# Moving the last step of the row statistics behind the next tile's work, and a segment's shifts to where the segment is loaded

## The chip, the cores and the metric

The kernel runs on one core of one Trainium2 chip. The core has five engines that run their own instruction queues side by side, each in the order in which its queue was filled: PE (TensorE, the matrix multiplies), DVE (VectorE), ACT (ScalarE), POOL (GpSimd) and SP (SyncE, which here issues most of the loads and stores between the chip's memory and the core). PE's partial sums lie in PSUM, whose banks DVE and ACT read and free; here eight banks are taken in turn. An engine that comes to an instruction whose input is not ready, or whose output space is not free, stands still, with everything behind it in its queue.

The metric is the device time of one execution in microseconds. Lower is better.

## The reference

Four layers work on one sequence of 2048 rows of 640 numbers, in the order A, B, A, B. Each reads the layer-normalised rows and adds its result to the rows:

```
def _layernorm(x):  m = mean(x); v = var(x); return (x - m) / sqrt(v + 1e-5)

x = x + _A_ref(_layernorm(x), A_wqkv, A_wo)
x = x + _B_ref(_layernorm(x), B_wq, B_wk, B_wv, B_wo, B_beta)
x = x + _A_ref(_layernorm(x), ...)
x = x + _B_ref(_layernorm(x), ...)
```

A is linear attention with 32 heads of 20: `phi(q) @ (sum of phi(k) v)` over all rows, divided by `phi(q) @ (sum of phi(k))`, and a projection with `wo`. B cuts the rows into four segments of 512: softmax attention within a segment under a causal mask, mixed by a gate with a linear-attention memory of the segments before it, and a projection. Of all this the change touches one thing, the layer normalisation of the rows that a layer has just written. With r = (v + 1e-5)^-0.5 a normalised row is x*r + (-m*r). The kernel calls r `rs`, the second term, the shift, `nb` (or `nb4` for four tiles at once), and the normalised tile `xh`.

## The kernel before, in words

A segment of 512 rows is worked on as four tiles of 128 rows. Only PE's order is written out by hand: Python generators are woven into one another, each yields a cost, and PE's instructions stand in the order in which the generators issued them. The orders of the other engines are set by a scheduler, which goes by the order of issue and by its own estimates of when things are ready. `issue_after(x)` makes what is issued under it, on the engine of instruction x, stand behind x.

*Layer A.* `g_first` builds keys, queries and memory, and `merge` folds the projections. For a segment, `a_head` prepares, and `a_second` then runs over the four tiles: it loads the old rows (`xo`, L340), multiplies the tile by the output weights in two halves of 15 matmuls (`o_half`, L406), and after each half DVE adds the old rows (`xn`, L483). When both halves are there, `moments` (L343 to L355) makes the statistics: DVE's two `bn_stats` (L348) and `bn_aggr` (L350), DVE's `rs = var + 1e-5` (L352), POOL's power -0.5 (L353), and DVE's `nb` (L355). `normed` lets ACT make `xh` (L378). Two tiles later `turn` transposes `xh` on PE (L329), and ACT (L333) and DVE (L334) copy it as a high and a low half into `xT`, the input of layer B. The turns of the last two tiles are the generator `tail`, which is woven into B's projections.

*Layer B.* `b_project` makes values (w_Bv, L406), queries and keys (w_Bq, w_Bk, L391; split by ACT L830 and DVE L831), `pkT` (DVE L431, turned on PE in L858) and the memory's sums (L868). Attention of the segments runs woven into all of this: scores with DVE's row maxima (PE L993, DVE L999), the maxima split and turned (L1008, L1009, L1017, ACT L1019, SP L1022), scores again for the exponentials (PE L1034, ACT L1038), weights times values (L1061) and normalisation (L1074, L1077). `p_read` brings A's prepared query tiles back (`pqi`, L744, L754 to L760) to be turned on PE.

`b_out` is B's counterpart of `a_second`. Here ACT scales a half (L480) and POOL adds the old rows (L481). When another layer follows, DVE's `gather` (L363, L364) takes the statistics of the tile before, after the last tile `settle` makes `rs` of the whole segment (DVE L370, POOL L371) and `nb4` (DVE L373), and `load_segment` later loads the four tiles again for the next layer's `g_norms`.

*Where the work stands.* Layer by layer, `a_second` of segment s is woven with B's memory work of segment s-1; segment s's projections are woven with the tail, with `a_head` of the next segment and, from s = 2 on, with `b_out` of segment s-2. In time, in the first pair of layers: `a_second` of segment 0 from 262 us, of segment 1 from 340 us, of segment 2 from 478 us and of segment 3 from 633 us; `b_out` of the four segments between 540 and 970 us. The second pair repeats the `a_second` part from 1092 us on, with no `b_out` that takes statistics, since no layer follows. So `nb` runs 36 times (4 in the opening, 32 in `a_second`), `nb4` 7 times (3 in the opening, 4 in `b_out`).

Of the kernel before, what the change touches and what calls it, by code (L numbers as in the profile page):

```python
# [9 lines left out]
F32 = mybir.dt.float32  # L10
# [4 lines left out]
OP = mybir.AluOpType  # L15
# [6 lines left out]
P = 128  # L22
C = D // P
SEG = 512
NSEG = S // SEG
NT = SEG // P
# [103 lines left out]
def pause(n):  # L130
    for _ in range(n):
        yield 0.0
# [12 lines left out]
class Kernel:  # L145
# [194 lines left out]
        self.nc.sync.dma_start(x, src[r:r + P])  # L340
        return x

    def moments(self, x):  # L343

        nc, sb = self.nc, self.sb
        st = sb.tile([P, 2, 6], F32, tag="st", name="st", bufs=3)
        for k in range(2):
            nc.vector.bn_stats(st[:, k], x[:, k * HN:(k + 1) * HN])  # L348
        mv = sb.tile([P, 2], F32, tag="mv", name="mv", bufs=4)
        nc.vector.bn_aggr(mv, st)  # L350
        rs = sb.tile([P, 1], F32, tag="rs", name="rs", bufs=4)
        self.taken = nc.vector.tensor_scalar(rs, mv[:, 1:2], 1e-5, None, op0=OP.add)  # L352
        self.power = nc.gpsimd.tensor_tensor(rs, rs, self.mhalf, op=OP.pow)  # L353
        nb = sb.tile([P, 1], F32, tag="nb", name="nb", bufs=4)
        self.last = nc.vector.tensor_scalar(nb, mv[:, 0:1], rs, -1.0, op0=OP.mult, op1=OP.mult)  # L355
        return x, nb, rs

    def gather(self, x, mv):
# [4 lines left out]
            nc.vector.bn_stats(st[:, k], x[:, k * HN:(k + 1) * HN])  # L363
        nc.vector.bn_aggr(mv, st)  # L364

    def settle(self, mv):

        nc, sb = self.nc, self.sb
        rs = sb.tile([P, NT], F32, tag="rs4", name="rs4", bufs=NSEG)
        nc.vector.tensor_scalar(rs, mv[:, :, 1], 1e-5, None, op0=OP.add)  # L370
        nc.gpsimd.tensor_tensor(rs, rs, self.mhalf.to_broadcast([P, NT]), op=OP.pow)  # L371
        nb = sb.tile([P, NT], F32, tag="nb4", name="nb4", bufs=NSEG)
        nc.vector.scalar_tensor_tensor(nb, mv[:, :, 0], -1.0, rs, op0=OP.mult, op1=OP.mult)  # L373
        return rs, nb

    def normed(self, x, nb, rs):
# [98 lines left out]
    def o_half(self, oT, wo, L, x, xn, n, later=False, begun=None):  # L475
        nc = self.nc
        p = self.proj_n(oT, wo, 0, n, begun, range(3, C)) if begun is not None else self.proj_n(oT, wo, 0, n)
        c = slice(n * HN, (n + 1) * HN)
        if later:
            nc.scalar.activation(xn[:, c], p, AF.Copy, scale=self.io[L])  # L480
            nc.gpsimd.tensor_tensor(xn[:, c], xn[:, c], x[:, c], op=OP.add)  # L481
        else:
            nc.vector.scalar_tensor_tensor(xn[:, c], p, self.io[L], x[:, c], op0=OP.mult, op1=OP.add)  # L483


    def parts(self, xh, xs, i):
# [7 lines left out]
    def norms(self, src, s, box, gap):  # L494

        x = [self.load_x(src, s, i) for i in range(NT)]
        mv = self.sb.tile([P, NT, 2], F32, tag="mv4", name="mv4", bufs=2)
        with self.tc.issue_after(self.keyed.ins) if s == 1 else nullcontext():
            for i in range(NT):
                self.gather(x[i], mv[:, i])  # L500
            rs, nb = self.settle(mv)
        box.append([(x[i], nb[:, i:i + 1], rs[:, i:i + 1]) for i in range(NT)])
        yield 0.0
        yield from pause(gap)
        yield from self.g_norms(s, box, 4 if s == 1 else 0)

    def load_segment(self, src, s, box, st):

        rs, nb = st["norm"]
        box.append([(self.load_x(src, s, i), nb[:, i:i + 1], rs[:, i:i + 1]) for i in range(NT)])  # L510
        yield 0.0

# [265 lines left out]
    def a_second(self, src, dst, s, L, box, norm):  # L778


        nc = self.nc
        o, oT = box["o"], box["oT"]
        xT = self.x_t() if norm else None
        xh = []
        for i in range(NT):
            if i + 3 < NT:
                yield from self.p_read(L, s, i + 3, o)
            x = self.load_x(src, s, i, "xo")
            xn = self.row("xn")
            t = iter(())  # L790
            if i + 1 < NT:
                oT.append(self.new_oT())
                t = self.turn(o[i + 1], oT[i + 1], 0)
            for n in range(2):
                yield from (c for c in [next(t, None)] if c)
                self.o_half(oT[i], L["wm"], "G", x, xn, n)
                yield self.COST_N
            r = s * SEG + i * P
            self.q_x.dma_start(dst[r:r + P], xn)
            if norm:  # L800
                if i > 1:
                    yield from self.turn(xh[i - 2], xT, i - 2)
                xh.append(self.normed(*self.moments(xn)))
        box["xT"] = xT

        def tail():
            for i in range(NT - 2, NT):
                yield from self.turn(xh[i], xT, i)
        box["tail"] = tail()


# [112 lines left out]
    def b_out(self, st, wo, src, dst, norm):  # L924

        yield lambda: st.get("attended")
        nc, s = self.nc, st["s"]
        made = []
        mv = self.sb.tile([P, NT, 2], F32, tag="mv4", name="mv4", bufs=2) if norm else None

        def load(i):
            if st["o"] is None and i < NT:
                read.append(self.row("ol"))
                nc.sync.dma_start(read[i], st["od"][i])

        def turned(i):
            load(i + 1)
            o = read[i] if st["o"] is None else st["o"][:, i]
            oT.append(self.new_oT())
            return self.turn(o, oT[i], 0)  # L940

        oT, read, begun = [], [], [None, None]
        load(0)
        t = turned(0)
        if st.get("ends"):
            ahead = turned(1)
            yield next(t)
            yield next(ahead)
            for n in range(2):
                begun[n] = self.proj_n(oT[0], wo, 0, n, cs=range(3))  # L950
                yield 9 * HN * COL
        yield from t
        for i in range(NT):
            x = self.load_x(src, s, i, "xo")
            xn = self.row("xn")
            t = iter(()) if i + 1 == NT else ahead if i == 0 and st.get("ends") else turned(i + 1)
            for n in range(2):
                yield from (c for c in [next(t, None)] if c)
                self.o_half(oT[i], wo, "B", x, xn, n, later=not st.get("ends"), begun=begun[n] if i == 0 else None)
                yield self.COST_N  # L960
            r = s * SEG + i * P
            self.q_x.dma_start(dst[r:r + P], xn)
            made.append(xn)
            if norm and i > 0:
                self.gather(made[i - 1], mv[:, i - 1])
        if norm:
            self.gather(made[-1], mv[:, NT - 1])
            st["norm"] = self.settle(mv)


    def stacks(self, st, g):
# [256 lines left out]
    def dense(self, layers, stage_ctx):  # L1228
# [15 lines left out]
        while i < n:  # L1244
# [35 lines left out]
            if last:  # L1280
                self.rate = R_END
                segs[-1]["ends"] = True
                yield from chain(fin, *out)
            else:
                self.rate = R_MID
                for k in "kq":
                    wA[k] = self.fetch(("A", k))
                L = self.g_begin(i + 2)
                src = xs[i + 2]
                x = [[] for _ in range(NSEG)]  # L1290
                loads = lambda s: self.load_segment(src, s, x[s], segs[s])
                norms = lambda s: self.g_norms(s, x[s])
                over = lambda st: lambda: st.get("attended")
                yield from weave(fin, chain(loads(0), norms(0)))
                use = lambda n: wA[n]
                yield from weave(self.g_first(0, x[0], use, L, over(segs[2])),
                                 chain(loads(1), when(segs[2], "attended", out[2]), norms(1)))
                yield from weave(self.g_first(1, x[1], use, L, over(segs[3])),
                                 chain(when(segs[3], "attended", out[3]), loads(2), norms(2)))
                yield from weave(self.g_first(2, x[2], use, L), chain(loads(3), pause(8), norms(3)))  # L1300
                wA["v"] = self.fetch(("A", "v"))
                yield from weave(self.g_first(3, x[3], use, L), self.a_head(L, 0, box))
# [63 lines left out]
```

## Time and profile before

| | us |
|---|---|
| median of three runs (lowest to highest) | 1705.25 (1703.31 to 1706.91) |
| the profiled execution | 1704.55 |
| its span | 1702.8 |
| PE busy | 1637.9 (96% of the span) |
| DVE busy | 1272.3 (75%) |
| ACT busy | 994.2 (58%) |
| POOL busy | 505.9 (30%) |

The span runs from the first to the last instruction in the trace; 1.75 us of the execution lie outside it. Row numbers such as L355 are lines of the kernel before. In a view of groups a row gives line, engine, operation, output<-input, count, then busy time, mean in ns of one, then the idle time of the engine just ahead of such instructions and what ended it. In a timeline a row gives start and duration in us, and in brackets the idle time ahead of it with what released it. In a table of stretches, a row gives the stretch, its length, and then busy time with the number of instructions for PE, PE's weight loads, DVE, ACT and POOL, the granted PE clock (1.00 is full speed), the share of time of the transfers and their GB/s.

### The profile page before, as it was taken

The page shows a single profiled execution, that of the slowest core. Times are in us where ns is not written, and L with a number is a line of the kernel's source. Part 1 is how long each engine was busy: PE and PEld are TensorE (multiplying, and loading weights), DVE is VectorE, ACT ScalarE, POOL GpSimd, SP SyncE. Part 2 cuts the span into 40 slices and gives each one's busy share as a digit, 9 for nine tenths or more (in the row PEclk, how much of TensorE's full clock was granted, in tenths as well). Part 3 has the DMA queues.
Part 4 walks back from the last instruction along what each step waited for, and adds up shares of the span by engine and source line. Part 5 has one row for each costly group of instructions (what it writes and reads, how often), then busy time and mean ns, then how long its engine had stood idle before and what let it go on. Part 6 is the DMA issues. An engine that isn't in the chain of part 4 may idle for free.

```text
span 1702.8 us, 37843 instructions
## 1 busy us (share of the span) xinstructions
PE 1637.9 (96%) x13788; PEld 1018.6 (60%) x13788; DVE 1272.3 (75%) x4015; ACT 994.2 (58%) x1888; POOL 505.9 (30%) x1046
## 2 busy tenths in 40 slices
PE   7999979999999999999999999999999999999998
PEld 5767757554465556556566777765546545645555
DVE  7888887487887788759874465847888978878773
ACT  6666533347756746667776454333675676666673
POOL 3442222013223322333452210310322332233452
PEclk9999989999999999999999999999999999999999
DMA  6424654421322331353211303423232323323432
GB/s 218 151 75 169 223 203 152 136 98 59 111 79 69 115 118 56 128 183 95 72 56 39 117 32 125 178 94 123 70 110 89 114 83 110 102 86 111 140 103 95
DMA packets 110372, 191.00 MB, mean 112 GB/s; under 512 B 14172, under 2 KB 69596, under 8 KB 107624
## 3 DMA queue, kind: packets, MB, share of 16 engines
q1 hardware_dynamic: 97704, 142.68, 25.9%
q0 software_dynamic: 3264, 24.91, 4.1%
q10 hardware_dynamic: 9216, 20.98, 3.2%
q8 instruction: 109, 1.79, 0.4%
q14 instruction: 79, 0.65, 0.1%
HBM read 109.32 MB, written 78.64 MB: 110 GB/s over the span
## 4 chain that ended last, share of the span: by engine, by line
PE 66%; DVE 17%; ACT 9%; issue 3%; DMA 3%; POOL 2%; SPq 0%; ACTq 0%; POOLq 0%; DVEq 0%
PE ps L406 25%; PE ps L391 13%; PE ps L1061 8%; PE ps L580 4%; PE ps L1034 4%; ACT pe L1038 3%; PE ps L993 3%; PE ps L329 3%; DVE ps L999 3%; PE ps L457 2%; PE ps L1074 1%; DVE e L421 1%; DVE wmx L243 1%; DVE split L270 1%; DVE xT L334 1%
## 5 line engine op out<-in xcount | busy, mean ns | idle before, releaser
L999 DVE CUSTOM_DVE_ANT_0 ps<-ps,maskw 128x512 f32<-128x512 f32 (+3 forms) x1024 | 472.0, 518 | 28.7 <-PE ps L993 25.9
L1038 ACT ACTIVATE pe<-ps,lsc 128x512 f32<-128x512 f32 x640 | 395.4, 696 | 63.0 <-PE ps L1034 59.8
L406 PEld LDWEIGHTS <-xT 128*128 128x128 f16 x2880 | 282.2, 99 | 115.0 <-issue 6.2
L1045 POOL TENSOR_SCALAR_AFFINE_SELECT pe<-pe 128x256 f32<-128x256 f32 (+1 forms) x640 | 233.4, 372 | 350.5 <-ACT pe L1038 342.7
L406 PEld LDWEIGHTS <-oT 128*128 128x128 f16 x1920 | 184.5, 98 | 84.7 <-issue 8.3
L1061 PE MATMUL ps<-pe,v 128*32 128x512 f32 (+3 forms) x2048 | 161.6, 436 | 8.8 <-DVE oT L334 1.9
L406 PE MATMUL ps<-wm,oT 128*128 128x320 f16 x960 | 141.3, 299 | 3.8 <-DVE rs L352 2.6
L406 PE MATMUL ps<-w_Bo,oT 128*128 128x320 f16 x960 | 141.5, 299 | 3.2 <-ACT oT L333 2.0
L406 PE MATMUL ps<-w_Ak,xT 128*128 128x320 f16 x960 | 140.6, 303 | 3.1 <-DVE xT L334 1.0
L406 PE MATMUL ps<-w_Bv,xT 128*128 128x320 f16 x960 | 142.3, 303 | 0.2
L391 PE MATMUL ps<-xT,w_Bq 128*128 128x512 f16 x600 | 140.9, 379 | 1.3 <-ACT pe L1038 0.8
L999 DVE DVE_READ_ACCUMULATOR2_ANT mg<- 128x1 f32 x1024 | 142.1, 139 | 0.1
L580 PE MATMUL ps<-pk,xs 128*128 128x321 f16 (+1 forms) x960 | 140.7, 304 | 1.1 <-DVE pk L543 0.7
L391 PE MATMUL ps<-xT,w_Bk 128*128 128x512 f16 x600 | 138.5, 379 | 1.2 <-ACT pe L1038 1.2
L406 PE MATMUL ps<-w_Aq,xT 128*128 128x320 f16 x960 | 137.6, 299 | 0.1
L993 PE MATMUL ps<-ks,qs 60*128 60x512 f16 (+3 forms) x1024 | 123.5, 297 | 7.6 <-ACT pe L1038 3.5
L580 PEld LDWEIGHTS <-xs 128*128 128x128 f16 x960 | 93.9, 99 | 41.0 <-issue 1.6
L421 DVE SCALAR_TENSOR_TENSOR e<-e,r 128x320 f32<-128x320 f32 x128 | 69.6, 544 | 53.6 <-ACT r L420 53.0
L1034 PE MATMUL ps<-qs,ks 62*128 62x512 f16 (+3 forms) x1024 | 105.6, 300 | 2.1 <-ACT pe L1038 1.1
L1061 PEld LDWEIGHTS ps<-pe,v 128*32 128x32 f32 x2048 | 65.4, 109 | 68.7 <-issue 40.9
L831 DVE SCALAR_TENSOR_TENSOR nat<-ps,nat 128x512 f16<-128x512 f32 x80 | 55.2, 690 | 62.6 <-ACT nat L830 62.3
L391 PEld LDWEIGHTS <-w_Bk 128*128 128x128 f16 x600 | 57.1, 98 | 66.5 <-issue 6.4
(202 smaller groups left out, 2359.6 us busy)
## 6 DMA issues: line engine op xcount, KB each, us to landing
x<-xn ACTq DMA_DIRECT2D x48, 320.0 KB
qs<-qd SPq DMA_DIRECT2D x128, 120.0 KB
ks<-kd SPq DMA_DIRECT2D x128, 120.0 KB
xo<-x SPq DMA_DIRECT2D x48, 320.0 KB
pqi<-pqd SPq DMA_DIRECT2D x32, 320.0 KB
qd<-nat SPq DMA_DIRECT2D x40, 256.0 KB
kd<-nat SPq DMA_DIRECT2D x40, 256.0 KB
x<-in_A_x SPq DMA_DIRECT2D x16, 320.0 KB
```

Of the source, the lines that this page charges most:

```text
L329: nc.tensor.transpose(pt[:, (c - c0) * P:(c - c0 + 1) * P], src[:, c * P:(c + 1) * P], self.ident)
L391: nc.tensor.matmul(p, w[:, c, a, t * P:(t + 1) * P], xT[:, c, b, :], start=k == 0, stop=k == 3 * C - 1)
L406: nc.tensor.matmul(p, xT[:, c, a, i * P:(i + 1) * P], w[:, c, b, n * HN:(n + 1) * HN], start=k == 0, stop=k == 3 * C - 1)
L421: nc.vector.scalar_tensor_tensor(e, e, 1.0, r, op0=OP.min, op1=OP.add)
L580: nc.tensor.matmul(p, xs[:, i, a, c * P:(c + 1) * P], pk[i][:, b, cols], start=i == 0 and a == b, stop=i == NT - 1 and a == 1)
L831: nc.vector.scalar_tensor_tensor(nat[:, 1], p, QK_SHIFT, nat[:, 0], op0=OP.mult, op1=OP.subtract)
L993: nc.tensor.matmul(bs[par][:, a:a + n], qs[r, p, i * P:(i + 1) * P], ks[r, p, :n], start=True, stop=True)
L999: nc.vector.tensor_tensor_reduce(bs[par][:, a:a + n], bs[par][:, a:a + n], self.maskw[:, SEG - n:], 1.0, NEG, OP.add, OP.max, G["mg"][:, p ...
L1034: nc.tensor.matmul(b[:, a:a + n], ks[r, p, j * P:(j + 1) * P], qs[r, p, j * P:], start=True, stop=True)
L1038: nc.scalar.activation(e, b, AF.Exp, scale=self.lsc)
L1045: nc.gpsimd.affine_select(d, d, pattern=pat, compare_op=OP.is_ge, fill=0.0, base=0, channel_multiplier=-1)
L1061: nc.tensor.matmul(G["pv"][32 * h4:32 * h4 + 32, j * P:], v[j][:, h * E1:h * E1 + 32], G.pop((p, par, j)), start=j == 0, stop=j == 2, skip ...
```

## The change

Three edits; no instruction is added or removed.

1. In `a_second`, `moments(xn, False)` stops ahead of the shift. The shift of tile i-1 is issued in tile i, after its first `o_half`, and queued on DVE behind that half's `xn` (L483); `xh` of tile i-1 follows it. The last tile's shift is queued behind the low half (L334) of the first part of tile 2's turn, in `tail`.
2. In `b_out`, `gather` of the tile before is queued behind the L334 that was issued last, and the generator yields once more, at no cost, ahead of the last `gather`. That moves what follows by a step of the weaving.
3. `settle` stops ahead of `nb4`, which `load_segment` issues when it loads the segment. The tile `mv4` gets four buffers for two, since it now lives until then.

```diff
-    def moments(self, x):
+    def moments(self, x, whole=True):
...
-        nb = sb.tile([P, 1], F32, tag="nb", name="nb", bufs=4)
-        self.last = nc.vector.tensor_scalar(nb, mv[:, 0:1], rs, -1.0, op0=OP.mult, op1=OP.mult)
+        return self.shift(x, mv, rs) if whole else (x, mv, rs)
+
+    def shift(self, x, mv, rs):
+        nb = self.sb.tile([P, 1], F32, tag="nb", name="nb", bufs=4)
+        self.last = self.nc.vector.tensor_scalar(nb, mv[:, 0:1], rs, -1.0, op0=OP.mult, op1=OP.mult)
         return x, nb, rs
...
-    def settle(self, mv):
+    def settle(self, mv, whole=True):
...
+        return self.shift_all(mv, rs) if whole else (mv, rs)
+
+    def shift_all(self, mv, rs):
+        nb = self.sb.tile([P, NT], F32, tag="nb4", name="nb4", bufs=NSEG)
+        self.nc.vector.scalar_tensor_tensor(nb, mv[:, :, 0], -1.0, rs, op0=OP.mult, op1=OP.mult)
         return rs, nb
...
-            nc.vector.scalar_tensor_tensor(xn[:, c], p, self.io[L], x[:, c], op0=OP.mult, op1=OP.add)
+            self.added = nc.vector.scalar_tensor_tensor(xn[:, c], p, self.io[L], x[:, c], op0=OP.mult, op1=OP.add)
...
-        rs, nb = st["norm"]
+        rs, nb = self.shift_all(*st["norm"])
...
                 self.o_half(oT[i], L["wm"], "G", x, xn, n)
+                if norm and i > 0 and n == 0:
+                    with self.tc.issue_after(self.added.ins):
+                        m = self.shift(*m)
+                    xh.append(self.normed(*m))
                 yield self.COST_N
...
-                xh.append(self.normed(*self.moments(xn)))
+                m = self.moments(xn, False)
         box["xT"] = xT
 
         def tail():
-            for i in range(NT - 2, NT):
-                yield from self.turn(xh[i], xT, i)
+            t = self.turn(xh[NT - 2], xT, NT - 2)
+            yield next(t)
+            with self.tc.issue_after(self.lower.ins):
+                m2 = self.shift(*m)
+            xh.append(self.normed(*m2))
+            yield from t
+            yield from self.turn(xh[NT - 1], xT, NT - 1)
...
             if norm and i > 0:
-                self.gather(made[i - 1], mv[:, i - 1])
+                with self.tc.issue_after(self.lower.ins):
+                    self.gather(made[i - 1], mv[:, i - 1])
         if norm:
+            yield 0.0
             self.gather(made[-1], mv[:, NT - 1])
-            st["norm"] = self.settle(mv)
+            st["norm"] = self.settle(mv, False)
```

The next two pieces show how this changes an engine's order. In the changed kernel the same instructions have higher line numbers: L355 is L358, L483 is L489, L999 is L1016, L378 is L384, L391 is L397, L868 is L883.

DVE, in `a_second` of segment 1, where its third tile (tile 2) is done and its fourth (tile 3) is under way. `mg` is where a row maximum is read out. Before:

```order
L334 TENSOR_TENSOR xT<-ps,xT 128x2x128
L348 BN_STATS st<-xn 128x6 x2
L350 BN_AGGR mv<-st 128x2
L999 ISA ps,mg<-ps,maskw 128x512
L999 ISA mg 128x1
L352 TENSOR_SCALAR rs<-mv 128x1
L999 ISA ps,mg<-ps,maskw 128x512
L999 ISA mg 128x1
L355 TENSOR_SCALAR nb<-mv,rs 128x1
L999 ISA ps,mg<-ps,maskw 128x384
```

And after:

```order
L334 TENSOR_TENSOR xT<-ps,xT 128x3x128
L334 TENSOR_TENSOR xT<-ps,xT 128x2x128
L348 BN_STATS st<-xn 128x6
L350 BN_AGGR mv<-st 128x2
L352 TENSOR_SCALAR rs<-mv 128x1
L489 SCALAR_TENSOR_TENSOR xn<-ps,ioG,xo 128x320
L358 TENSOR_SCALAR nb<-mv,rs 128x1
L1016 ISA ps,mg<-ps,maskw 128x512
L1016 ISA mg 128x1
L1016 ISA ps,mg<-ps,maskw 128x512
```

The first half's `xn` of tile 3 now stands ahead of the eight row maxima; before, it stood behind all of them. The shift `nb` of tile 2 follows it. The same holds in the second pair of layers.

PE, in `b_project` of segment 2, where `b_out` of segment 0 ends and `a_head` of segment 3 begins to turn `pqi`. Before:

```order
L868 MATMUL ps<-v_87,pkt 32x63 x4
L868 MATMUL ps<-v_88,pkt 32x63 x4
L329 MATMUL ps<-ident,pqi 128x128 x3
L391 LDWEIGHTS w_Bq
L391 MATMUL ps<-xT,w_Bq 128x512
```

And after:

```order
L883 MATMUL ps<-v_86,pkt 32x63 x4
L883 MATMUL ps<-v_87,pkt 32x63 x4
L883 MATMUL ps<-v_88,pkt 32x63 x4
L397 LDWEIGHTS w_Bq
L397 MATMUL ps<-xT,w_Bq 128x512
```

And, nine matmuls further on:

```order
L397 LDWEIGHTS w_Bq
L397 MATMUL ps<-xT,w_Bq 128x512
L329 MATMUL ps<-ident,pqi 128x128 x3
L397 LDWEIGHTS w_Bq
L397 MATMUL ps<-xT,w_Bq 128x512
```

The turn of `pqi` has moved behind the first nine w_Bq matmuls. Its second part, two transposes, moved likewise, to just ahead of L858's. PE's order differs at one more place, near 960 us, where the first part of a turn of `xh` stands one place later. On the other engines orders shift as follows from this: ACT's copies of `oT` and some exponentials stand ahead of an `xh` that they stood behind, and SP issues the fourth tile's `xo` ahead of L1022's pair of small stores.

More of the change, by code (lines that the diff above doesn't have):

```diff
@@ L371, in settle @@
         nc.gpsimd.tensor_tensor(rs, rs, self.mhalf.to_broadcast([P, NT]), op=OP.pow)
-        nb = sb.tile([P, NT], F32, tag="nb4", name="nb4", bufs=NSEG)
-        nc.vector.scalar_tensor_tensor(nb, mv[:, :, 0], -1.0, rs, op0=OP.mult, op1=OP.mult)
+        return self.shift_all(mv, rs) if whole else (mv, rs)
+    def shift_all(self, mv, rs):
+        nb = self.sb.tile([P, NT], F32, tag="nb4", name="nb4", bufs=NSEG)
+        self.nc.vector.scalar_tensor_tensor(nb, mv[:, :, 0], -1.0, rs, op0=OP.mult, op1=OP.mult)
         return rs, nb
@@ L496, in norms @@
         x = [self.load_x(src, s, i) for i in range(NT)]
-        mv = self.sb.tile([P, NT, 2], F32, tag="mv4", name="mv4", bufs=2)
+        mv = self.sb.tile([P, NT, 2], F32, tag="mv4", name="mv4", bufs=NSEG)
         with self.tc.issue_after(self.keyed.ins) if s == 1 else nullcontext():
@@ L928, in b_out @@
         made = []
-        mv = self.sb.tile([P, NT, 2], F32, tag="mv4", name="mv4", bufs=2) if norm else None
+        mv = self.sb.tile([P, NT, 2], F32, tag="mv4", name="mv4", bufs=NSEG) if norm else None
         def load(i):
```

## The prediction

> **What bounds the kernel now.** I read the page first, then DVE's groups for what the moved instructions cost there, then a table of stretches for what PE loses where they stand, then the timelines of the places where it loses most.
>
> ```profile
> span 1702.8 us, 37843 instructions
> PE 1637.9 (96%) x13788; PEld 1018.6 (60%) x13788; DVE 1272.3 (75%) x4015; ACT 994.2 (58%) x1888; POOL 505.9 (30%) x1046
> ```
>
> PE is idle for 1702.8 - 1637.9 = 64.9 us of the whole span. Nothing the change does can win more, unless PE itself runs faster.
>
> ```profile
> L363 DVE BATCH_NORM_STATS2 st<-xn 128x6 f32<-128x320 f32 x32 | 15.7, 492 | 39.0 <-POOL xn L481 38.1 <-POOL pk L552 0.9
> L355 DVE TENSOR_SCALAR nb<-mv,rs 128x1 f32<-128x1 f32 x36 | 7.6, 212 | 20.2 <-POOL rs L353 19.4 <-POOL pk L551 0.7
> ...
>   POOL rs L371: 6.9, 7
> ```
>
> The third row is from the view of L373, what it waited for. Here DVE stands for POOL, at three kinds of instruction: 38.1 + 19.4 + 6.9 = 64.4 us. These are the waits that the change is aimed at. It would be wrong to book them as gain: that they are nearly PE's idle time is chance, since DVE is busy 75% and its standing costs only where PE then stands too. So the next view is PE's, by stretch.
>
> ```profile
> core 0: us, PE busy (x) PEld busy (x) DVE busy (x) ACT busy (x) POOL busy (x), PEclk, DMA share, GB/s
> 262.00:314.00 52.00, 51.57 (x378) 34.55 (x376) 28.28 (x67) 17.20 (x36) 7.90 (x9) 1.00 0.37 127
> 340.00:364.00 24.00, 22.16 (x197) 15.68 (x196) 21.68 (x82) 6.84 (x14) 1.64 (x3) 1.00 0.30 100
> 364.00:371.00 7.00, 5.90 (x46) 3.15 (x43) 5.33 (x19) 4.31 (x8) 2.12 (x5) 1.00 0.54 192
> 371.00:378.00 7.00, 6.64 (x48) 3.38 (x52) 5.81 (x20) 4.61 (x10) 2.48 (x6) 0.76 0.01 2
> 478.00:506.00 28.00, 27.37 (x267) 18.96 (x266) 24.80 (x96) 15.66 (x29) 6.37 (x18) 1.00 0.24 79
> 540.00:620.00 80.00, 74.98 (x659) 39.55 (x661) 60.24 (x194) 50.48 (x93) 30.20 (x55) 1.00 0.36 116
> 695.00:760.00 65.00, 63.44 (x474) 33.01 (x473) 43.64 (x159) 43.42 (x77) 24.58 (x53) 1.00 0.44 141
> 805.00:885.00 80.00, 77.93 (x695) 47.63 (x694) 64.25 (x234) 57.02 (x108) 33.98 (x70) 1.00 0.23 72
> ...
> 1200.00:1207.00 7.00, 6.21 (x39) 3.20 (x42) 5.30 (x19) 5.42 (x12) 2.94 (x8) 0.76 0.01 4
> ```
>
> Segment 0's `a_second` (262 to 314) leaves PE idle 0.43 us, segment 2's (478 to 506) 0.63; segment 1's (340 to 371) 1.84 + 1.10 = 2.94, followed by a stretch at a lower clock. The stretches of `b_out` leave 5.02, 1.56 and 2.07.
>
> **Edit 1 in segment 1.** This is PE there, then DVE, ACT and SP; the last two PE rows are the same place in the second pair of layers.
>
> ```profile
> 355.35 2.48 PE L406 MATMUL ps<-wm,oT 128*128 128x320 f16 x15
> ...
> 360.21 2.20 PE L406 MATMUL ps<-wm,oT 128*128 128x320 f16 x15 [1.31 <-DVE rs L352]
> ...
> 369.13 0.63 PE L1034 MATMUL ps<-qs,ks 62*128 62x384 f16 x6 [0.49 <-DVE mg L999]
> 369.94 0.27 PE L993 MATMUL ps<-ks,qs 60*128 60x256 f16 x1 [0.18 <-ACT pe L1038]
> 370.51 0.38 PE L993 MATMUL ps<-ks,qs 60*128 60x256 f16 x3 [0.31 <-ACT pe L1038]
> 371.22 0.44 PE L329 MATMUL ps<-ident,xh 128*128 128x128 f32 x2 [0.33 <-ACT v L435]
> 371.80 3.87 PE L406 MATMUL ps<-w_Bv,xT 128*128 128x320 f16 x15
> ...
> 1190.42 2.20 PE L406 MATMUL ps<-wm,oT 128*128 128x320 f16 x15 [1.31 <-DVE rs L352]
> ...
> 1202.00 3.50 PE L406 MATMUL ps<-w_Bv,xT 128*128 128x320 f16 x15
> ```
>
> ```profile
> 357.05 0.54 DVE L483 SCALAR_TENSOR_TENSOR xn<-ps,ioG,xo 128x320 f32<-128x320 f32 x1
> ...
> 359.42 0.67 DVE L999 CUSTOM_DVE_ANT_0 ps<-ps,maskw 128x512 f32<-128x512 f32 x1
> 360.01 0.14 DVE L999 DVE_READ_ACCUMULATOR2_ANT mg<- 128x1 f32 x1
> ...
> 364.62 1.00 DVE L483 SCALAR_TENSOR_TENSOR xn<-ps,ioG,xo 128x320 f32<-128x320 f32 x2
> ...
> 367.57 0.21 DVE L355 TENSOR_SCALAR nb<-mv,rs 128x1 f32<-128x1 f32 x1 [0.73 <-POOL rs L353]
> ...
> 367.82 0.92 ACT L378 ACTIVATE xh<-xn,nb,rs 128x640 f32<-128x640 f32 x1 [1.11 <-DVE nb L355]
> ...
> 359.62 0.34 SPq L340 DMA_DIRECT2D xo<-in_A_x  x1
> ```
>
> Tile 3's first half ends on PE at 355.35 + 2.48 = 357.83, but DVE takes its sum only at 364.62, behind the row maxima. Its second half waits 1.31 us, to 360.21. The row names `rs`, which has nothing to do with that matmul; what ended just ahead of it is the first 512-wide maximum (360.01 + 0.14), which frees a PSUM bank. After the change the first half's sum stands ahead of the maxima (the order shown above). DVE also arrives earlier, without the waits for the shift (0.73 each where they stand alone, as at 367.57), so the sum can start at 357.83 and ends, at 0.54, near 358.4. A bank is free then, while PE is still in the small matmuls that ended at 358.90 (360.21 - 1.31). That gap goes.
>
> The four gaps behind it (0.49 + 0.18 + 0.31 + 0.33 = 1.31) hang on DVE's next maxima and on exponentials that stood on ACT behind `xh`, which waited 1.11 for the shift. After the change the shift and its wait are gone from ahead of those maxima, and those exponentials stand ahead of `xh`; these gaps go too. What is late next: the last `xh` now starts only behind the low half of tile 2's turn, and the copy that frees the bank for the turn's second part (L435) stands behind it. I price that as one `xh`, 0.92, rounded to 1.0. So 1.31 + 1.31 - 1.0 = 1.6 per pair of layers, 3.2 for two. Bounds: nothing, if a new wait takes all of it, and 2 x 2.62 = 5.2.
>
> **The clock.** Right behind these gaps the w_Bv group takes 3.87 where its like takes 2.20 (the 2.20 of the other L406 rows, 15 matmuls too), and 3.50 the second time, with a granted clock of 0.76 over 371 to 378 and over 1200 to 1207. That is 1.67 + 1.30 = 3.0 us. It follows 1.31 us of idle time in the 2.67 us ahead of 371.80, cut into four pieces, among small matmuls; the single gap of 1.31 at 358.90, among full ones, had no such effect. With the four pieces gone, or one of 1.0 left, I take the lower clock to go: 3.0. Bounds: 0, and 3.0. If drops go by a phase that the shifted start changes, one can come elsewhere at the same 1.7; that is the second rival.
>
> [...]
>
> **Edit 1 elsewhere.** In segment 0 and in segments 2 and 3 the same moves are made. PE lost 0.43 and 0.63 there, so at most some 0.6 per segment can be won, and I book nothing. What hides the later `xh`: its turn comes two tiles later. But DVE is busy 24.80 of 28 in segment 2, so a sum moved ahead of the maxima could make them late. The place where it is tightest:
>
> ```profile
> 495.75 2.20 PE L406 MATMUL ps<-wm,oT 128*128 128x320 f16 x15
> ...
> 497.92 0.21 DVE L355 TENSOR_SCALAR nb<-mv,rs 128x1 f32<-128x1 f32 x1 [0.68 <-POOL rs L353]
> ...
> 499.67 0.55 DVE L483 SCALAR_TENSOR_TENSOR xn<-ps,ioG,xo 128x320 f32<-128x320 f32 x1
> ```
>
> The sum moves ahead of the first maxima at a cost of 0.55 and takes the shift's wait of 0.68 out from there; its matmuls end at 497.95, when DVE would come to it. That cancels. SP now issues the fourth `xo` ahead of L1022's stores; it went out at 359.62 and would have to be there at 357.83, so it must go out earlier, which its new place allows once the first `xh` has freed a row. I book 0, with 0.6 up or down per segment, six of them: -3.6 to +3.6.
>
> **Edits 2 and 3.** PE loses most in segment 0's `b_out`:
>
> ```profile
> 600.80 0.55 PE L329 MATMUL ps<-ident,pqi 128*128 128x128 f32 x3 [1.05 <-POOL pqi L760]
> ...
> 606.11 0.66 PE L858 MATMUL ps<-ident,pkT 128*128 128x128 f32 x4 [1.31 <-DVE pkT L431]
> ...
> 601.76 0.16 DVE L373 SCALAR_TENSOR_TENSOR nb<-mv,rs 128x4 f32<-128x4 f32 x1 [1.63 <-POOL rs L371]
> ```
>
> The extra step of the weaving puts the turn of `pqi` behind nine w_Bq matmuls, so its 1.05 us have time to pass. `nb4`, whose wait of 1.63 stood on DVE ahead of the chain to `pkT`, is gone from there; of that 1.31 I take 1.0, as ACT feeds the chain too. Sum 2.05. `gather`'s 38.1 us fall where PE loses little, and I book nothing for it. Bounds: 0 and the 5.02 + 1.56 + 2.07 = 8.7 that PE is idle in these stretches. The second pair has no such `b_out`. `nb4` at the load waits for nothing: its power is long done.
>
> **Sum.** 1704.55 - 3.2 - 3.0 - 2.05 = 1696.3 for an execution like the profiled one, which is 0.70 under the median of the runs: 1697.0.
>
> **Rivals.** What can be told from no change is 0.2%, 3.4 us.
>
> - *Hidden.* PE's gaps come back a few us later at the next thing that is late: DVE, at 21.68 of 24 before 364, sets the pace of row maxima, and a maximum that starts earlier waits for the next. Then only the 2.05 of `b_out` and little else stay: 1702 to 1706, say 1703.5. For it: DVE's share here and that no work leaves it. Against: the two gaps hang on an order, not on DVE's sum of work.
> - *The clock stays low, or falls elsewhere.* 3.0 less: 1700.0.
> - *Slower: the sum ahead of the maxima.* DVE works strictly in its order. Where the first half's sum now stands ahead of the maxima and PE's half or the load of `xo` is late, the maxima, the exponentials and PE's next scores stand behind it. In the six segments with maxima there are three such places each. At 18 places one sum of 0.54 each is 9.7; with the 2.05 of `b_out` won and segment 1's gaps kept, 1705.25 + 9.7 - 2.05 = 1712.9. It decides from 5.5 / 18 = 0.3 us a place. Against it: at 497.95 the matmuls are just in time.
> - *The change doesn't do what it says.* The shift's wait goes only if POOL is done by the time of its new place. POOL's power and its way took 0.73 behind `rs`, and a sum of 0.54 stands between: some waits stay at 0.2. That is small, and lies within the case "hidden".
>
> **Chances.** The sum (1692 to 1699) 0.46, clock low 0.19, hidden 0.20, slower 0.15. Hidden splits into 0.04 below 1701.85 and 0.16 above. Faster: 0.46 + 0.19 + 0.04 = 0.69; same 0.16; slower 0.15. The range leaves out the slower case beyond 1708 and a sum with most of `b_out`'s bound: 1691 to 1708. The likeliest case's own range is 1692 to 1699.
>
> **What would show it.** Right: PE's L406 of tile 3 in segment 1 without its 1.31, in both pairs of layers; w_Bv groups of 2.20 and a clock of 1.00 near 371 and 1201; POOL rs L353 nearly gone from what L358 waits for; the turn of `pqi` near 601 without its wait. Wrong: new PE waits for DVE's maxima (L1034, or the row maxima's L993) in segments 2 and 3, DVE waiting for PE or for `xo` at the sum (L489), or a clock drop at a new place.

## The result

| | us |
|---|---|
| before, median of 20 runs (lowest to highest) | 1704.90 (1702.75 to 1709.40) |
| after, median of 20 runs | 1701.72 (1699.46 to 1704.54) |
| ratio, with its 95% interval | 0.9981 [0.9975, 0.9988] |

The changed kernel is 3.2 us faster (2.0 to 4.3 by the interval). The forecast was 1697.0, 8 us faster: the sign was right, and the time lies in the range, but the gain is less than half of what was forecast. The time lies above the case of the sum (1692 to 1699), between the rival with the low clock (1700.0) and the hidden one (1703.5). Of the executions below, one of edit 1 alone (6259.79 us) and two of before (2059.03 and 1736.77 us) stood far off and are in no ratio.

The first lines of the page of the changed kernel, three of DVE's groups, and behind them the table of stretches, with one more stretch than was shown of before:

```profile
span 1698.7 us, 37836 instructions
PE 1634.8 (96%) x13788; PEld 1015.6 (60%) x13788; DVE 1267.9 (75%) x4015; ACT 993.4 (58%) x1888; POOL 505.5 (30%) x1046
...
L489 DVE SCALAR_TENSOR_TENSOR xn<-ps,ioG,xo 128x320 f32<-128x320 f32 x64 | 35.1, 549 | 18.3 <-PE ps L412 17.7
L366 DVE BATCH_NORM_STATS2 st<-xn 128x6 f32<-128x320 f32 x32 | 15.0, 487 | 19.5 <-POOL xn L487 19.5
L358 DVE TENSOR_SCALAR nb<-mv,rs 128x1 f32<-128x1 f32 x36 | 7.4, 206 | 3.9 <-POOL rs L353 3.1 <-POOL pk L557 0.7
```

In before, the first of these groups was:

```profile
L483 DVE SCALAR_TENSOR_TENSOR xn<-ps,ioG,xo 128x320 f32<-128x320 f32 x64 | 34.1, 544 | 4.8 <-PE ps L406 4.5
```

The stretches of the changed kernel:

```profile
340.00:364.00 24.00, 23.58 (x212) 16.60 (x210) 23.04 (x85) 8.40 (x17) 1.94 (x4) 1.00 0.32 96
364.00:371.00 7.00, 5.91 (x56) 3.64 (x57) 5.71 (x24) 6.25 (x14) 3.24 (x8) 1.00 0.47 173
371.00:378.00 7.00, 6.99 (x70) 3.99 (x64) 7.00 (x24) 3.70 (x8) 1.57 (x3) 1.00 0.27 75
478.00:506.00 28.00, 27.30 (x268) 17.22 (x267) 24.22 (x90) 16.43 (x32) 6.93 (x18) 1.00 0.19 66
540.00:620.00 80.00, 77.02 (x692) 41.85 (x692) 63.80 (x207) 51.31 (x94) 28.85 (x53) 1.00 0.38 122
695.00:760.00 65.00, 63.65 (x469) 33.32 (x469) 42.73 (x151) 42.09 (x75) 22.40 (x48) 1.00 0.48 155
805.00:885.00 80.00, 75.79 (x671) 45.94 (x672) 62.63 (x230) 55.57 (x106) 34.78 (x69) 1.00 0.21 68
1200.00:1207.00 7.00, 7.00 (x68) 4.50 (x61) 7.00 (x23) 4.16 (x8) 2.21 (x3) 1.00 0.23 71
1640.00:1644.00 4.00, 3.12 (x14) 1.94 (x14) 3.52 (x13) 3.31 (x7) 1.92 (x5) 0.60 0.06 24
```

DVE's waits for POOL went as the change means them to: 19.4 to 3.1 us at the shift and 38.1 to 19.5 at the gathers. At `nb4` little went: 6.9 to 5.3. Of its four places in `b_out`, where it waited 1.63, 1.15, 0.62 and 0.74, only the first is rid of its wait; the others wait 1.15, 0.61 and 0.74 still. DVE now stands for PE instead, 17.7 us at the sum (L489; before, 4.5). None of that says what PE won. PE's stretches do: segment 1 is denser (340 to 364: 23.58 busy, before 22.16), and the clock of 0.76 at 371 and 1200 is gone. But 805 to 885 has become worse (4.21 idle, before 2.07), and there is a low clock at 1640 that was not in the trace of before.

Segment 1 in the changed kernel, PE's timeline:

```profile
354.43 2.20 PE L412 MATMUL ps<-wm,oT 128*128 128x320 f16 x15
...
357.59 2.21 PE L412 MATMUL ps<-wm,oT 128*128 128x320 f16 x15
...
365.59 0.61 PE L1051 MATMUL ps<-qs,ks 62*128 62x384 f16 x8
366.04 0.39 PE L1010 MATMUL ps<-ks,qs 60*128 60x256 f16 x4
366.36 0.44 PE L329 MATMUL ps<-ident,xh 128*128 128x128 f32 x2
367.72 2.20 PE L412 MATMUL ps<-w_Bv,xT 128*128 128x320 f16 x15 [0.92 <-ACT v L441]
```

The 1.31 us ahead of the second half is gone, the four gaps behind it are gone, and one new wait stands there: 0.92, for ACT's copy L441, the wait that the prediction priced at 1.0.

PE runs the same 13,788 matmuls in nearly the same order in all these kernels, so the start of the k-th matmul can be laid against that in the trace of before. The difference, in us from each trace's first matmul, read at a place given by the time in before (minus is earlier; the last four columns are experiments below):

| place | after | before again | edit 1 alone | no gather move | segment 1 alone |
|---|---|---|---|---|---|
| 262 | -0.87 | -0.03 | +1.83 | +0.12 | +0.13 |
| 375 | -5.63 | -1.62 | -2.94 | -4.63 | -4.63 |
| 392 | -4.78 | -1.41 | -2.08 | -3.77 | -3.78 |
| 590 | -4.82 | -1.11 | -1.71 | -3.27 | -3.19 |
| 620 | -6.95 | -1.11 | -1.71 | -5.40 | -3.20 |
| 845 | -6.20 | -1.11 | -0.69 | -4.28 | -3.18 |
| 900 | -3.80 | -1.12 | -0.31 | -3.64 | -3.24 |
| 1180 | -3.57 | -1.12 | -0.31 | -3.39 | -2.96 |
| 1206 | -8.00 | -2.41 | -4.75 | -7.82 | -7.40 |
| 1222 | -7.11 | -2.12 | -3.87 | -6.93 | -6.52 |
| 1480 | -6.02 | -0.83 | -3.15 | -6.65 | -6.18 |
| 1640 | -5.38 | -0.85 | -2.47 | -6.42 | -6.22 |
| 1690 | -3.98 | +0.72 | -2.47 | -6.40 | -6.22 |

At 262, ahead of the first `a_second`, the traces already stand -0.87 to +1.83 against before. After that the changed kernel wins 4.8 us up to 375, 2.1 between 590 and 620, and 4.4 up to 1206. It loses 0.9 behind each of the segment 1 places, 0.8 between 620 and 845, 2.4 between 845 and 900, 1.7 between 1222 and 1640 (segments 2 and 3 of the second pair, and the last layer), and 1.4 at 1640.

### The profile page after: what moved, and what is told of

Same layout as the page of the kernel before. It is cut to its first block, busy times and chain, and to the rows that moved or that the text cites. A ratio compares the mean times of both kernels' runs of the same rounds, so it can differ in the third digit from the quotient of the medians.

```text
span 1698.7 us, 37836 instructions
## 1 busy us (share of the span) xinstructions
PE 1634.8 (96%) x13788; PEld 1015.6 (60%) x13788; DVE 1267.9 (75%) x4015; ACT 993.4 (58%) x1888; POOL 505.5 (30%) x1046
## 5 line engine op out<-in xcount | busy, mean ns | idle before, releaser
L1016 DVE CUSTOM_DVE_ANT_0 ps<-ps,maskw 128x512 f32<-128x512 f32 (+3 forms) x1024 | 472.1, 521 | 42.5 <-PE ps L1010 40.2
L1078 PE MATMUL ps<-pe,v 128*32 128x512 f32 (+3 forms) x2048 | 166.2, 436 | 7.8 <-POOL pe L1062 2.2
L1016 DVE DVE_READ_ACCUMULATOR2_ANT mg<- 128x1 f32 x1024 | 145.2, 142 | 0.0
L397 PE MATMUL ps<-xT,w_Bq 128*128 128x512 f16 x600 | 140.9, 380 | 1.3 <-ACT pe L1055 0.8
L397 PE MATMUL ps<-xT,w_Bk 128*128 128x512 f16 x600 | 138.5, 379 | 1.2 <-ACT pe L1055 1.2
L1051 PE MATMUL ps<-qs,ks 62*128 62x128 f16 (+3 forms) x1024 | 105.0, 300 | 1.1 <-ACT pe L1055 1.1
L397 PEld LDWEIGHTS <-w_Bk 128*128 128x128 f16 x600 | 57.1, 98 | 66.3 <-issue 6.2
```

The lines of the kernel that those rows point to most:

```text
L397: nc.tensor.matmul(p, w[:, c, a, t * P:(t + 1) * P], xT[:, c, b, :], start=k == 0, stop=k == 3 * C - 1)
L1016: nc.vector.tensor_tensor_reduce(bs[par][:, a:a + n], bs[par][:, a:a + n], self.maskw[:, SEG - n:], 1.0, NEG, OP.add, OP.max, G["mg"][:, p ...
L1051: nc.tensor.matmul(b[:, a:a + n], ks[r, p, j * P:(j + 1) * P], qs[r, p, j * P:], start=True, stop=True)
L1078: nc.tensor.matmul(G["pv"][32 * h4:32 * h4 + 32, j * P:], v[j][:, h * E1:h * E1 + 32], G.pop((p, par, j)), start=j == 0, stop=j == 2, skip ...
```

## The experiments

Two accounts were set against each other. *Given back*: the wins are there, and the moved gathers lose them again near 855 us. *Clock by chance*: the lower clock that the prediction booked as won was not in most executions of before.

**Before again.** No edit.

> The kernel before once more, unchanged. Two accounts of why the gain was smaller than forecast. 'Given back': the change wins in segment 1 and at 600 us about what was forecast and loses 2 to 3 us in segment 2's b_out near 855 us, because the moved gathers make ACT's copies of oT stand behind four exponentials. [...] Given back expects the drop at both places again, about 371 and 1201. Clock by chance expects it to be missing at one or both. Time ratio 1.000 plus or minus 0.001 for both.

Ratio 1.000 [0.999, 1.001]. The lower clock was not at 371 or 1201 but at 1348.7 and 1645.6 (0.79 over 1345 to 1353, 0.72 over 1643 to 1649). The order of the instructions and the gaps near 371 were the same as in before. The second account is right on this point.

**Edit 1 alone.** The edits of `moments`, `shift` and `a_second` of the change's diff, nothing in `b_out`, `settle` or `load_segment`.

> Edit 1 alone (the shifts of a_second). Given back: segment 1's gains in both pairs of layers stay (the profile shows 4.9 and 4.4 won, 1.3 of each lost again right behind, so 3.1 to 3.6 each if the clock drop belongs to before), 850 to 878 us as in before: 6 to 7 us faster, ratio 0.9960 to 0.9965. Clock by chance: only the gaps are won, 1.7 to 2 each: 3 to 4 us, ratio 0.9976 to 0.9982.

0.9982 [0.9974, 0.9991], the value of clock by chance. The number alone misleads here: the run of segment 1 alone, further down, shows that edit 1 wins more than this and gives some of it back in segments 2 and 3.

**Edits 2 and 3.** The rest of the diff, without edit 1.

> Edits 2 and 3 without edit 1. Given back: 2.3 us won at 600 us by the extra step, 2 to 3 lost near 855: ratio 0.9995 to 1.0005, and the profile shows ACT's exponentials ahead of the copies of oT near 855 and PE waits there (0.49, 0.31, 0.63 in the changed kernel). Clock by chance: 2.3 us won and nothing lost: ratio 0.9985 to 0.9990.

1.0009 [0.9999, 1.0018]: the win at 600 us is lost again, as the first account has it (laid against before, the trace wins 2.1 us between 590 and 620 and loses 2.5 between 845 and 900). The two accounts are both true in part.

**No gather move.** The changed kernel, with this undone:

```diff
             if norm and i > 0:
-                with self.tc.issue_after(self.lower.ins):
-                    self.gather(made[i - 1], mv[:, i - 1])
+                self.gather(made[i - 1], mv[:, i - 1])
```

> The changed kernel with the gathers of b_out left in their old place (edit 1, the extra step of edit 2, edit 3). Given back: the loss near 855 goes, so 2 to 3 us faster than the changed kernel: ratio to before 0.9963 to 0.9970. Clock by chance: as the changed kernel, 0.9975 to 0.9988.

0.9961 [0.9948, 0.9974], 1698.02 us. By the two ratios to before that is 3.4 us faster than the changed kernel, a little more than the 2 to 3 that were expected.

**The gathers alone.** Before, with the two lines that the last diff takes out.

> Only the move of b_out's gathers behind the last low half (no extra step, no edit 1, no edit 3). If the moved gathers are what costs: 2.5 to 3 us lost between 850 and 880 us and nothing elsewhere, ratio 1.0015 to 1.0018. If it takes the extra step together with them: ratio 1.000. [...]

1.0016 [1.0004, 1.0028]: the moved gathers cost 2.7 us by themselves. The trace has the loss between 845 and 900 (2.3 us later there; before again, nothing), and no lower clock at all after 262 us. The queues of PE and ACT near that place show what happens; first of before, then of the changed kernel, where all is 6.4 us earlier:

```profile
843.56 0.55 PE L329 MATMUL ps<-ident,otok 128*128 128x128 f32 x3
...
846.46 0.52 ACT L333 ACTIVATE oT<-ps 128x384 f16<-128x384 f32 x1
...
856.26 0.38 PE L329 MATMUL ps<-ident,otok 128*128 128x128 f32 x2
...
856.89 0.52 ACT L420 ACTIVATE r<-ps,inv_Aq 128x320 f32<-128x320 f32 x1
857.30 0.38 ACT L333 ACTIVATE oT<-ps 128x256 f16<-128x256 f32 x1
...
859.55 2.42 ACT L1038 ACTIVATE pe<-ps,lsc 128x512 f32<-128x512 f32 x4
```

```profile
837.31 0.55 PE L329 MATMUL ps<-ident,otok 128*128 128x128 f32 x3
...
849.85 0.38 PE L329 MATMUL ps<-ident,otok 128*128 128x128 f32 x2
...
853.30 0.27 PE L1010 MATMUL ps<-ks,qs 60*128 60x256 f16 x1 [0.49 <-ACT r L426]
853.88 0.38 PE L1010 MATMUL ps<-ks,qs 60*128 60x256 f16 x3 [0.31 <-ACT pe L1055]
...
857.83 0.63 PE L1010 MATMUL ps<-ks,qs 60*128 60x384 f16 x4 [0.63 <-DVE oT L334]
...
853.14 2.42 ACT L1055 ACTIVATE pe<-ps,lsc 128x512 f32<-128x512 f32 x4
856.70 0.77 ACT L333 ACTIVATE oT<-ps 128x384 f16<-128x384 f32 x2 [1.13 <-PE ps L412]
...
862.98 0.94 ACT L486 ACTIVATE xn<-ps,ioB 128x320 f32<-128x320 f32 x2 [1.36 <-DVE st L366]
```

PE turns the same `otok` in both, in two parts, and ACT copies each part out of a PSUM bank. Before, the copies started 2.90 us (843.56 to 846.46) and 1.04 us (856.26 to 857.30) after their turns. Now both stand behind four exponentials, and the first waits 1.13 more, until a half of w_Bo on PE has ended: 19.39 us (837.31 to 856.70) and 7.23 us (849.85 to 857.08, the second copy of the row at 856.70). Until then the two results hold two of the eight banks, and PE waits 0.49 + 0.31 and then 0.63. The wait of 0.63 is ended by the low half (L334) of these very copies. For the other two a want of banks is likely, but their rows name other instructions. Further on ACT stands 1.36 us for a gather (`st`), since it may not write the next `xn` before. That the scheduler put the copies back because it reckoned with this wait fits, but no run shows it.

**The extra step alone.** Before, with `yield 0.0` ahead of the last gather.

> Only the extra step of the weaving in b_out. It should win the 2.1 us near 600 us (the turn of pqi without its 1.05 wait, L858 without its 1.31) and lose nothing near 855: ratio 0.9986 to 0.9990. If the earlier start is used up later, 0.9995 to 1.000. [...]

1.0000 [0.9991, 1.0010]: a miss for the expectation. PE's timeline of this run:

```profile
600.59 0.49 PE L329 MATMUL ps<-ident,pqi 128*128 128x128 f32 x3
...
604.96 0.66 PE L858 MATMUL ps<-ident,pkT 128*128 128x128 f32 x4 [2.37 <-DVE pkT L431]
605.45 5.08 PE L391 MATMUL ps<-xT,w_Bk 128*128 128x512 f16 x15
```

The wait for `pqi` is gone, and `pkT` waits 2.37 in its place: 1.05 + 1.31 before, 2.37 now. DVE makes `pkT` when it did before, whatever PE does: its wait for `nb4` ahead of it is 1.63 us here too. (In this execution the longer wait was followed by a lower clock, 0.71 over 604 to 609: 5.08 for fifteen matmuls that took 3.40 in before.)

**Edit 3 alone.** Before, with `nb4` given out when the segment is loaded.

> Only edit 3: nb4 given out when the segment is loaded. The extra step alone moved the 1.05 us wait at 600 us into L858, which then waited 2.37 for pkT; with edit 3 it waits 1.00. If DVE's wait for nb4 ahead of pkT is the cause, edit 3 alone takes L858's 1.31 down to nearly nothing and leaves the 1.05 of pqi: about 1.3 us won near 606, ratio 0.9992 with an interval that holds 1.000. If only both together win, L858 still waits 1.0 or more. Clock after 262 us: one to three lower stretches, as in the kernels whose segment 1 is as before.

0.9989 [0.9980, 0.9998], 1.9 us at the middle of a wide interval. PE's timeline (L861 is L858 of before):

```profile
602.90 0.55 PE L329 MATMUL ps<-ident,pqi 128*128 128x128 f32 x3 [1.04 <-POOL pqi L763]
...
606.98 0.66 PE L861 MATMUL ps<-ident,pkT 128*128 128x128 f32 x4
...
616.20 0.65 PE L861 MATMUL ps<-ident,pkT 128*128 128x128 f32 x4 [1.40 <-DVE pkT L434]
```

The first turn of `pkT` does not wait, as expected, and the trace is 1.2 us earlier there. Then the second waits 1.40 where before waited 0.56, and 0.4 us is left at 620. With step and edit 3 together, in the changed kernel, there is one wait, and 2.1 us stay:

```profile
599.79 0.66 PE L873 MATMUL ps<-ident,pkT 128*128 128x128 f32 x4 [1.00 <-DVE pkT L437]
```

By the traces the two edits win together what neither wins alone.

**Segment 1 and the step.** As the run without the gather move, and edit 1 in segment 1 only:

```diff
-                if norm and i > 0 and n == 0:
+                if norm and s == 1 and i > 0 and n == 0:
...
-                m = self.moments(xn, False)
+                m = self.moments(xn, s != 1)
+                if s != 1:
+                    xh.append(self.normed(*m))
...
-            with self.tc.issue_after(self.lower.ins):
-                m2 = self.shift(*m)
-            xh.append(self.normed(*m2))
+            if s == 1:
+                with self.tc.issue_after(self.lower.ins):
+                    m2 = self.shift(*m)
+                xh.append(self.normed(*m2))
```

> Edit 1 in segment 1 only, the extra step, edit 3, gathers left in place. If the later xh in segments 2 and 3 costs about 0.65 at each of four places (xh stands between two exponentials that PE's L1061 matmuls wait for), this is 2 to 3 us faster than the run without the gather move: ratio to before 0.9943 to 0.9952. If that loss is only PE's earlier start running into work that is as late as ever, it is the same as that run: 0.9958 to 0.9965.

0.9951 [0.9935, 0.9967], 1697.44 us. By time it can't be told from the run with edit 1 in all segments (0.9961).

**Segment 1 alone.** The same edit without the rest.

> Edit 1 in segment 1 only, nothing else. The gaps of 2 x 1.7 net, less about 0.3 lost behind each: 2.8 us; with the lower clock of 371 and 1201 no longer possible, which before has in about half of the executions each, 1.6 more: 4 to 5 us, ratio 0.9971 to 0.9977. If segments 2 and 3 cost nothing, the same as edit 1 whole: 0.9982.

0.9961 [0.9946, 0.9976], 1698.79 us: more than was expected, and more than edit 1 whole (0.9982), though the intervals just touch. The traces agree: from 262 us on edit 1 whole wins 1.83 + 2.47 = 4.3, segment 1 alone 0.13 + 6.22 = 6.35. So edit 1 costs some 2 us in segments 2 and 3. One place of it, at the start of segment 2, in before and in the changed kernel, ACT and then PE:

```profile
488.24 0.92 ACT L378 ACTIVATE xh<-xn,nb,rs 128x640 f32<-128x640 f32 x1 [1.73 <-DVE nb L355]
...
489.77 1.26 ACT L1038 ACTIVATE pe<-ps,lsc 128x512 f32<-128x512 f32 x2 [0.24 <-PE ps L1034]
...
491.16 1.48 PE L1061 MATMUL ps<-pe,v 128*32 128x384 f32 x24
```

```profile
484.85 0.69 ACT L1055 ACTIVATE pe<-ps,lsc 128x512 f32<-128x512 f32 x1 [2.85 <-PE ps L1051]
485.44 0.91 ACT L384 ACTIVATE xh<-xn,nb,rs 128x640 f32<-128x640 f32 x1
486.25 0.67 ACT L1055 ACTIVATE pe<-ps,lsc 128x512 f32<-128x512 f32 x1
...
486.02 2.13 PE L1078 MATMUL ps<-pe,v 128*32 128x384 f32 x24
```

The later shift puts `xh` between two exponentials. The matmuls that follow, which take the exponentials (`pe`), need 2.13 instead of 1.48: 0.65, without any wait shown between the groups, since it lies inside the group. With edit 1 in segment 1 only the row is 1.48 again. Laid against each other, the traces of edit 1 whole and of segment 1 alone show this step, of about 0.6, at the start of segments 2 and 3 of both pairs, and further on smaller ones of both signs.

**The last shift later.** As segment 1 and the step, with the last tile's shift behind the second part of the turn:

```diff
             yield next(t)
+            yield from t
             if s == 1:
                 with self.tc.issue_after(self.lower.ins):
                     m2 = self.shift(*m)
                 xh.append(self.normed(*m2))
-            yield from t
```

> The run with edit 1 in segment 1, the extra step and edit 3, with one more edit: the last tile's shift goes behind the low half of the second part of tile 2's turn, not the first, so that ACT's xh stands behind the copy L441. If xh ahead of that copy is what PE waits 0.92 for, that wait goes in both pairs of layers: 1.8 us faster than that run at most, ratio to before 0.994 to 0.9948. If DVE's pace takes it back, no change: 0.995. Clock after 262 us: none or one.

0.9956 [0.9943, 0.9968], no change to 0.9951. PE's 0.92 for the copy L441 is gone, and near 386 the trace is 1.8 us ahead of the run of segment 1 and the step; by 389 it is 0.3 ahead. Among what takes it back are 24 matmuls that take 2.25 where they took 1.48, and a wait for POOL's mask behind ACT's exponentials:

```profile
368.28 2.20 PE L412 MATMUL ps<-w_Bv,xT 128*128 128x320 f16 x15
...
372.36 2.25 PE L1080 MATMUL ps<-pe,v 128*32 128x384 f32 x24
...
387.92 0.99 PE L1080 MATMUL ps<-pe,v 128*32 128x256 f32 x8 [0.55 <-POOL pe L1064]
```

What PE wins in segment 1 beyond this is taken back within some 20 us, at matmuls that take the exponentials.

**The gathers, but not in segment 2.**

```diff
-                with self.tc.issue_after(self.lower.ins):
+                with self.tc.issue_after(self.lower.ins) if s != 2 else nullcontext():
                     self.gather(made[i - 1], mv[:, i - 1])
```

> The changed kernel with the gathers left in their old place in segment 2 only. If the whole loss of the moved gathers is in segment 2's b_out (850 to 880 us), this is 2.5 to 3.5 us faster than the changed kernel, ratio to before 0.9958 to 0.9968, with no PE waits of 0.49, 0.31 and 0.63 there. If it lies in other segments too, it stays nearer 0.998.

0.9964 [0.9951, 0.9977], 1697.47 us, and no waits of 0.49, 0.31 and 0.63 near 855. As far as times can tell, the whole loss of the gathers is in segment 2's `b_out`. (The profiled execution of this run alone was held up for 7.6 us near 760 us, where ACT waited 5.7 for a transfer of `kd`; its other times were not.)

**The changed kernel again.**

> The changed kernel once more, beside the two others on one chip. Ratio to before 0.998, with the loss between 850 and 880 us; lower clock after 262 us at most once or twice, and not at 371 or 1201.

0.9979 [0.9970, 0.9988], with the same waits near 855. The lower clock after 262 us came once, at 1642.8 (0.88 over 1636 to 1650).

**The clock over all runs.** Where the granted clock was low (1.00 elsewhere) after 262 us, in the one trace of each run:

| segment 1 as before | | edit 1 in segment 1 | |
|---|---|---|---|
| before | 371, 1201 | after | 1641 |
| before again | 1349, 1646 | after again | 1643 |
| edits 2 and 3 | 372, 1646 | edit 1 alone | none |
| gathers alone | none | no gather move | none |
| step alone | 371, 606 | segment 1 and step | 1639 |
| edit 3 alone | 374, 1203 | segment 1 alone | none |
| | | last shift later | 1639 |

(The run of the gathers outside segment 2 is left out for its disturbance.) Ten in six traces on the left, four in seven on the right. A place that has the gaps is hit in one execution and not in the next.

What decides it, no run shows. The gaps ahead of the w_Bv group near 371 are 0.49, 0.18, 0.31 and 0.33 us in all six traces on the left (0.34 for the last with edit 3 alone). The group behind them takes 3.71 to 3.87 us in four of the six, and 2.20 in the two others, before again and the gathers alone. With edit 1 in segment 1 one wait of 0.92 or 0.93 is left there, with the last shift later none, and the group takes 2.20 in all seven. Near 1640 before and the changed kernel have the same gaps, 0.51, 0.20 and 0.86; a low stretch followed in the changed kernel (0.60 over 1640 to 1644) and none in before (1.00 over 1644 to 1652). And idle time alone does not tell: the single gap of 1.31 near 358, among full matmuls, is in all six traces on the left, and the group behind it takes 2.20 in each.

A larger sample is the mean granted clock that is listed for each execution: 0.9929 over 92 of before and 0.9936 over 31 of the changed kernel. The part that is missing to 1, times the length of the execution, is 12.1 and 10.8 us. An estimate from these of what the change won by the clock in all is 1.3 us if PE was busy in all of that time, less if not, give or take 0.9.

## Why the prediction was right or wrong

**The gaps of segment 1: the mechanism right, the size too small.** It was booked as 1.6 a pair of layers, 3.2 in all. The first sum moved ahead of the maxima, the 1.31 went, the four small gaps went, and the new wait was 0.92. The trace shows 4.76 won up to 375 and 4.43 up to 1206, but before's trace happened to have a low clock at both places. Laid against before again, which had none there, it is 3.2 and 3.1, and 2.5 each after what is lost again behind: 5.1 for 3.2 booked, near the upper bound of 5.2. The gaps between small matmuls cost more than the brackets say: from the first of the small matmuls to the w_Bv group it was 371.80 - 368.25 = 3.55 in before and is 367.72 - 365.59 = 2.13, so 1.42 won where the brackets give 1.31 - 0.92 = 0.39. In before they begin with this row:

```profile
368.25 0.39 PE L1034 MATMUL ps<-qs,ks 62*128 62x384 f16 x2
```

The 0.6 that is lost again behind each fits DVE's pace, which the prediction named as a rival: DVE is busy 7.00 of 7.00 us from 371 to 378.

**The clock: 3.0 booked, less than half of it there.** The step that failed is reading the trace's two low stretches as the standing cost of these gaps. In six traces with these gaps the place near 371 was hit four times and the one near 1201 twice: 6 of 12, so 1.5 of the 3.0 on average. That the change takes it away at these two places holds in all seven traces with edit 1 in segment 1. The second rival had it that a drop could come elsewhere, and one near 1640 came in four of these seven, and in two of the six without. The gaps there are the same before and after; this is the changed kernel:

```profile
1638.87 0.37 PE L1051 MATMUL ps<-qs,ks 62*128 62x384 f16 x2 [0.51 <-ACT pe L1055]
1639.44 0.40 PE L1051 MATMUL ps<-qs,ks 62*128 62x384 f16 x4 [0.20 <-ACT pe L1055]
...
1641.25 0.90 PE L329 MATMUL ps<-ident,otok 128*128 128x128 f32 x3 [0.86 <-ACT pe L1055]
1641.95 3.30 PE L412 MATMUL ps<-w_Bo,oT 128*128 128x320 f16 x15
```

By the estimate from the granted clocks of all executions, about 1 of the 3.0 was there to win.

**`b_out`: 2.05 booked, 2.1 found, but not by the parts named.** The prediction added 1.05 for the step and 1.0 for `nb4`. Alone, the step wins nothing and `nb4` 0.4 by the trace. Only together do they win 2.1, so that the number came out right is luck. "`nb4` at the load waits for nothing" holds at the first of four places only.

**The gathers: booked at nothing, cost 2.4 by the trace and 2.7 to 3.4 by the ratios.** This is the step whose failure cost most. "`gather`'s 38.1 us fall where PE loses little" looked for a gain and bounded it from below with 0. It should have asked what the moved reads hold up on ACT: the order of ACT's copies and exponentials in segment 2's `b_out` changes with the gathers, and so do the banks that the copies free.

**Edit 1 elsewhere: booked at 0, with 0.6 a segment either way; cost some 2.** "What hides the later `xh`: its turn comes two tiles later" is right of PE's turn and wrong of ACT: a later `xh` takes 0.92 of ACT between two exponentials that PE needs sooner. The bound held (-3.6 to +3.6), its middle did not.

**The slower rival** did not come about as told. DVE does stand at the sum, 17.7 us where it stood 4.5, but PE's waits for the maxima did not grow: 4.0 us in the whole trace of before, 3.3 in that of the changed kernel.

Added up, from these: 5.1 for segment 1, about 1 for the clock and 2.1 for `b_out` are 8.2, as much as was forecast. That is luck, since the first is 1.9 above its term and the second about 2 below. 2.4 for the gathers and some 2 for segments 2 and 3 are given back. That leaves 3.8; the runs say 3.2. The parts come from one trace each, and the clock's from means that differ by little.

The gain is to be had: the runs without the gathers' move, or with edit 1 in segment 1 only, are 6.6 to 8.4 us faster than before (0.9961 to 0.9951). Among themselves they can't be told apart.

## What to carry to other kernels

Of an instruction that is moved later on one engine, ask of each engine behind it which instruction it will now stand ahead of, and which buffer it holds longer: both losses here came from ACT. One came by an `xh` that moved along with its shift, the other by copies that no edit touches. A price that a single trace shows at one place, above all of the clock, may be chance until a second trace has it. And where two waits stand one behind the other in front of the same engine, taking one away alone may win nothing.

## What was not expected of the hardware

The same gaps, in the same order of instructions, were followed by a low stretch in some executions and not in others: at 371 and 1201 in 6 of the 12 cases that the six traces without edit 1 in segment 1 hold, and near 1640 in 6 of the 13 traces of the table. It took no long gap: in the changed kernel the low stretch at 1641 came behind 0.51, 0.20 and 0.86 us of idle time among small matmuls, and in before the same three gaps, from 1644 on, came ahead of none. In the low stretches at 371.8 and 1201.3 in before and at 1640.8 in the changed kernel the granted clock was 0.50, for 3.4 us each. One low stretch cost 1.3 to 1.7 us (3.50 and 3.87 for fifteen matmuls that take 2.20 elsewhere, 5.08 for fifteen that take 3.40).
